# Placing the on-chip buffers of a four-layer kernel at multiples of 256 bytes

## The chip, the cores and the metric

The kernel runs on one core of one Trainium2 chip. The metric is device time in microseconds (us) from launch to end; of several runs of a kernel the median is taken. Beside it stands the profile of one execution, in which TensorE is called PE (its weight loads PEld), VectorE DVE, ScalarE ACT, GpSimd POOL, and SyncE SP. SP issues nearly all of the transfers.

## The reference

Four layers follow one another on one sequence of 2,048 rows of 640 numbers: A, B, A, B, each added to its input.

```python
x = A_x
x = x + _A_ref(_layernorm(x), A_wqkv, A_wo)
x = x + _B_ref(_layernorm(x), dft_seq_re, dft_seq_im, dft_hid_re, dft_hid_im)
x = x + _A_ref(_layernorm(x), A_wqkv, A_wo)
x = x + _B_ref(_layernorm(x), dft_seq_re, dft_seq_im, dft_hid_re, dft_hid_im)

# A: 32 heads of 20 numbers; each row looks at 8 rows: itself and 2, 4, ... 14 back
qkv = x @ wqkv                        # 640 -> 1920
logits = q . k[pos - 2 * (0..7)] * scale     # masked where pos - 2w < 0
y = softmax(logits) @ v[...] ; y @ wo        # 640 -> 640

# B: real part of a two-dimensional Fourier transform, as matrix products
a = x @ dft_hid_re.T ; b = x @ dft_hid_im.T
y = dft_seq_re @ a - dft_seq_im @ b
```

## The kernel before, in words

The sequence is cut into 4 chunks (`NC`) of 128 partitions by 4 rows (`NJ`). All matrix products are done at close to full float32 accuracy on a faster, shorter float format: each operand is split into a high part and a low part, and each product is three matmuls, high by high, high by low, low by high (`PASSES`, L222). Every matmul loads its own stationary operand (128 columns) and then streams a moving operand of 320, 480 or 512 columns past it.

Layer A (`layer_a`, L246) is a plan of steps: `at(step, phase, ...)` collects calls, and at the end they are written out step by step on all five engines in the order of `PHASES` (`manual_schedule`, so that order is the order of issue). PE computes Q, K and V for one group of rows in `qkv_mm` (L356): 15 matmuls of 480 columns, with the transposed input (tag `s0` to `s3`, one for each row j) as stationary operand and the weights of a quarter of the heads (tag `r1_0` to `r1_3`, one for each quarter q) as moving operand. The weights of a quarter are a tile `[P, 2, KD, 3 * F]`: high and low, 5 blocks of 128 inputs, 480 numbers in each. ACT copies the result out, SP stores it, and loads it again with the seven rows before it into `win` buffers. DVE does the attention: `qk_mul` (L432), `qk_red` (L442), `soft` (L455), `av_mul` (L473); POOL halves sums for it (L438, L494 to L496). The output projection is `wo_mm` (L510, matmuls at L519, 320 columns).

Layer B (`LayerB`, L892) first multiplies by the sequence matrix and then by the hidden one. The normalised rows stand as high and low parts in `self.xn[c]`, a tile `[P, 2, NJ, D]` for each chunk c in the tags `r1_0` to `r1_3`. `z_mm` (L971, matmuls at L982) makes the first of eight output tiles, at the end of layer A, and `zpart` the second at the start of layer B: `xn` is stationary and a column block of the sequence matrix (tags `s0` to `s3`, 512 columns) moves. The other six tiles are made two by two in `pair` (L1169) with seven products in place of eight (Strassen's scheme) in three loops of eight steps; `product` (L1158, matmuls at L1161) issues three passes of 512 columns for each of one or two banks. Its stationary operand comes from `x_plain` or `x_slot` (one of the chunks of `xn`); its moving operand is one of the `views`: the first part of `xn[2]`, `xn[3]` (tags `r1_2`, `r1_3`) or `s0`, `s1`. In the first loop one step is 18 matmuls; steps 0, 1, 4 and 5 take the stationary operand of two of their three products from chunk 0 (`r1_0`), steps 2, 3, 6 and 7 from chunk 1 (`r1_1`); the third product takes it from `r1_2` or `r1_3`. `ymm` (L1053, matmuls at L1064, 320 columns) multiplies by the hidden matrix: stationary `zo0`, `zo1`, `zo2`, `ot`; moving `r2a` (real part) and `pr0` to `pr3`, `zo3` (imaginary part). In `pair` the order on PE is written out; the other engines' order comes from a planner with a cost model that knows no addresses.

The buffers. `T(shape, tag)` asks one pool for a tile. Tiles of one tag share one place (or as many as `bufs` says), as large as the tag's largest tile. The pool lays the tags out in the order in which each is first asked for, each rounded up to 32 bytes of a partition. In the compiled program of the kernel before, scratch, constants, `warm`, `ident` and `nident` take the first 17,568 bytes of each partition, and the tags begin at these bytes:

| tags in order | first byte | remainder by 256 |
|---|---|---|
| ident, nident | 16544, 17056 | 160 |
| s3 | 17568 | 160 |
| mhalf, mask | 22688, 22720 | 160, 192 |
| r1_0, pr0 | 22784, 43264 | 0 |
| win, five buffers of 3,520 bytes | 48384 and on | 0, 192, 128, 64, 0 |
| pr1, pr2, pr3, r1_1, r2a, r1_2, r1_3 | 65984 to 147904 | 192 |
| zo2, zo3, ot | 168384 to 178624 | 192 |
| stats (8 of 64 bytes), junk | 183744 and on | (not read by PE) |
| s0, s1, stg (2), s2, zo0, zo1, qs, xa (2), lg (2), xr | 185536 to 226752 | 192 |

The last tag ends at byte 229,312. Every slice that PE reads begins at a multiple of 512 or 1,280 bytes inside its buffer and so has the remainder of its buffer, with one exception: the 480 numbers of a block of QKV weights are 1,920 bytes, seven and a half times 256, so that every second block is shifted by 128: in `r1_0` the blocks have the remainders 0 and 128 in turn, in `r1_1` to `r1_3` 192 and 64.

Of the kernel before, what the change touches and what calls it, by code (L numbers as in the profile page):

```python
# [11 lines left out]
F32R = mybir.dt.float32r  # L12
# [14 lines left out]
P = 128  # L27
# [2 lines left out]
NQ = 4  # L30
KD = D // P
F = 160
HQ = 8
NE = 8
FE = 80
# [20 lines left out]
NWIN = 5  # L56
# [16 lines left out]
SLOTS = NJ + W - 1  # L73
ROWS = W - 1 + S // 2
PAIRED = {NE * (NC - 1) + v: (v % NQ, v // NQ) for v in range(NE)}


@with_exitstack
def tile_layers(ctx: ExitStack, tc: tile.TileContext, x, wqkv, wo, cs, wre, wim, out):
# [10 lines left out]
    def nm(base):  # L90
        uid[0] += 1
        return f"{base}_{uid[0]}"

    def T(shape, tag, dt=F32, bufs=1, pool=None):
        return (pool or sb).tile(shape, dt, tag=tag, name=nm(tag), bufs=bufs)
# [8 lines left out]
    make_identity(nc, ident)  # L104
    nident = T([P, P], "nident", F32R)
    nc.scalar.activation(nident, ident, AF.Copy, scale=-1.0)
    zero = T([P, D], "s3", mybir.dt.bfloat16)
    nc.vector.memset(zero, 0.0)
    wb = pt([P, 512], "m1")
    for i in range(NWARM):  # L110
        nc.tensor.matmul(wb, zero[:, :P], zero[:, :512], start=True, stop=True)
    mhalf = T([P, 4], "mhalf")
    nc.gpsimd.memset(mhalf, -0.5)
    mask = T([P, SLOTS], "mask")
    nc.gpsimd.memset(mask, 0.0)
    nc.gpsimd.memset(mask[0:2, 0:3], NEG)
    nc.gpsimd.memset(mask[0:1, 3:7], NEG)
# [11 lines left out]
    def split(hi, lo, src, neg=False, eng=None):  # L129
        nc.scalar.activation(hi, src, AF.Copy, scale=-1.0 if neg else 1.0)  # L130
        if neg:
            nc.vector.scalar_tensor_tensor(lo, src, -1.0, hi.bitcast(F32), op0=ALU.mult, op1=ALU.subtract)
        else:
            (eng or nc.vector).tensor_tensor(lo, src, hi.bitcast(F32), op=ALU.subtract)
# [68 lines left out]
    def wtile(shape):  # L203
        return T(shape, "win", bufs=NWIN)

    def wq_load(q, k0, k1, tag):
        raw = T([P, k1 - k0, 3 * F], tag)
        nc.sync.dma_start(raw, wqkv[q][:, k0:k1, :])
        return raw

    def wq_load1(q, k):
        raw = wtile([P, 3 * F])
        nc.sync.dma_start(raw, wqkv[q][:, k, :])
        return raw

    def a_weights_q(q):
        wt = T([P, 2, KD, 3 * F], f"r1_{q}", F32R)
        for k in range(KD):
            split(wt[:, 0, k], wt[:, 1, k], wq_load1(q, k))
        return wt  # L220
# [25 lines left out]
    def layer_a(li, stats, handoff, prev):  # L246
# [4 lines left out]
        wq = {}  # L251
# [5 lines left out]
        qs = {}  # L257
        win = {}
# [5 lines left out]
        xr = {}  # L264
# [91 lines left out]
        def qkv_mm(g, cqj):  # L356
# [4 lines left out]
            for a, b in PASSES:  # L361
                for k in range(KD):
                    if n == (10 if g < 2 else 5):
                        for fn, args in mid.pop(g, ()):
                            fn(*args)
                    nc.tensor.matmul(mt[g][:, : 3 * F], st[:, a, k], wq[q][:, b, k], start=n == 0, stop=n == 14)  # L366
                    n += 1

        def qkv_evac(g, cqj):
            c, q, j = cqj  # L370
            if j % 2 == 0:
                sgs[q] = T([P, 6, 2, FE], "stg", bufs=2)
            nc.scalar.copy(sgs[q][:, :, j % 2], mt.pop(g)[:, : 3 * F].rearrange("p (a f) -> p a f", f=FE))  # L373

# [167 lines left out]
            nstats[c].finish(j0, j1)  # L542

        def wq_begin(q):
            wq[q] = T([P, 2, KD, 3 * F], f"r1_{q}", F32R)

        def wq_raw(q):
            if q < 3:
# [15 lines left out]
        def wq_late(q, k):  # L564
            if k == 0:
                wq_begin(q)
            wq[(q, k)] = wq_load1(q, k)
# [23 lines left out]
        def early():  # L591
# [4 lines left out]
            def w0():  # L596
                with tc.issue_after(prev.dma.ins):
                    wq[0] = a_weights_q(0)
# [32 lines left out]

        def prologue_first():
            wq_begin(0)
            for j, (k0, k1) in enumerate(((0, 3), (3, 5))):
                x_load(0, j, f"pr{j}")
# [4 lines left out]
            for q in (1, 2, 3):  # L640
                wq_begin(q)
                wq_raw(q)
# [753 lines left out]
```

## Time and profile before

| | |
|---|---|
| time, median of 3 runs | 1762.35 us (1760.95 to 1767.62) |
| span of the profiled execution, first to last instruction | 1757.1 us |
| PE, DVE, ACT, POOL busy | 1731.3, 1375.7, 807.6, 621.2 us |
| matmuls | 8,798: 1,920 at L366 (480 columns), 1,920 at L1064 and 960 at L519 (320), 2,592 at L1161 and 960 at L982 (512), the rest transposes and warm-up |
| transfers | 426.20 MB, mean 243 GB/s |

The profiled execution lies 5.2 us under the median of the runs, because a span leaves out what lies before the first and after the last instruction. The layers lie in it at about 0 to 404 us (A, its last part already belongs to B's first tile), 404 to 870 us (B), 870 to 1273 us (A) and 1273 to 1757 us (B).

A matmul's duration in the profile runs to the modelled end of its results, and one begins before the one ahead of it has ended. What a matmul costs in a stream is therefore the time from its start to the next one's start, called its pitch here: the distance of two start times in the timeline over the number of matmuls between them.

### The profile page before, as it was taken

The page shows a single profiled execution, that of the slowest core. Times are in us where ns is not written, and L with a number is a line of the kernel's source. Part 1 is how long each engine was busy: PE and PEld are TensorE (multiplying, and loading weights), DVE is VectorE, ACT ScalarE, POOL GpSimd, SP SyncE. Part 2 cuts the span into 40 slices and gives each one's busy share as a digit, 9 for nine tenths or more (in the row PEclk, how much of TensorE's full clock was granted, in tenths as well). Part 3 has the DMA queues.
Part 4 walks back from the last instruction along what each step waited for, and adds up shares of the span by engine and source line. Part 5 has one row for each costly group of instructions (what it writes and reads, how often), then busy time and mean ns, then how long its engine had stood idle before and what let it go on. Part 6 is the DMA issues. An engine that isn't in the chain of part 4 may idle for free.

```text
span 1757.1 us, 26454 instructions
## 1 busy us (share of the span) xinstructions
PE 1731.3 (99%) x8798; PEld 1501.6 (85%) x8798; DVE 1375.7 (78%) x2131; ACT 807.6 (46%) x1682; POOL 621.2 (35%) x585
## 2 busy tenths in 40 slices
PE   9999999989999999999999999989999999999999
PEld 7889897868888888888998899978788888888888
DVE  6999999988667767767648999989887677677673
ACT  4664544554445445445534434444434443443441
POOL 4799998940000000000028998889200000000000
PEclk9999999999999999999999999999999999999999
DMA  8996769759777777787657866798687767767761
GB/s 286 311 325 207 225 200 334 264 174 306 257 262 249 244 254 239 235 272 227 195 178 235 269 205 211 223 328 279 205 313 260 253 197 261 256 208 237 262 202 53
DMA packets 273961, 426.20 MB, mean 243 GB/s; under 512 B 22656, under 2 KB 153728, under 8 KB 273568
## 3 DMA queue, kind: packets, MB, share of 16 engines
q1 hardware_dynamic: 270624, 422.54, 72.7%
q10 hardware_dynamic: 3200, 1.97, 0.4%
q8 instruction: 70, 1.15, 0.3%
q14 instruction: 67, 0.55, 0.1%
HBM read 339.28 MB, written 85.14 MB: 242 GB/s over the span
## 4 chain that ended last, share of the span: by engine, by line
PE 83%; DVE 7%; DMA 4%; POOL 3%; issue 2%; ACT 1%; SPq 0%; DVEq 0%; ACTq 0%; POOLq 0%
PE m L366 20%; PE aux L1064 16%; PE t L1161 11%; PE m L1161 11%; PE pq L1161 6%; PE xt L1161 6%; PE aux L519 4%; PE t L982 3%; PE m L982 3%; DVE pr L475 2%; DMA win<-kvb 2%; PE xt L982 2%; DVE pr L435 1%; DVE lg L445 1%; POOL pr L494 1%
## 5 line engine op out<-in xcount | busy, mean ns | idle before, releaser
L366 PE MATMUL m<-r,s 128*128 128x480 f32 x1920 | 436.2, 381 | 0.7 <-DVE r L649 0.2
L366 PEld LDWEIGHTS m<-r,s 128*128 128x128 f32 x1920 | 355.5, 188 | 54.4 <-DVE r L649 1.0
L1064 PE MATMUL aux<-r2a,zo 128*128 128x320 f32 x768 | 226.6, 310 | 0.0
L1154 ACT CAST r<-win 128x512 fp32r<-128x512 f32 x246 | 149.9, 620 | 163.2 <-DVE win L1190 84.7
L494 POOL TENSOR_TENSOR pr<-pr 128x640 f32<-128x640 f32 x126 | 205.8, 1633 | 33.2 <-DVE pr L475 33.0
L1064 PE MATMUL aux<-pr,zo 128*128 128x320 f32 x704 | 208.3, 308 | 0.0
L178 POOL TENSOR_TENSOR stats<-stats,mhalf 128x1 f32<-128x1 f32 (+1 forms) x40 | 29.5, 737 | 493.4 <-ACT stats L174 484.5
L1155 DVE TENSOR_TENSOR r<-win,r 128x512 fp32r<-128x512 f32 x246 | 165.7, 688 | 45.2 <-ACT r L1154 44.1
L435 DVE TENSOR_TENSOR pr<-pq,win 128x1280 f32<-128x1280 f32 x128 | 189.8, 1483 | 13.9 <-DMA win<-kvb 8.0
L475 DVE TENSOR_TENSOR pr<-pq,win 128x1280 f32<-128x1280 f32 x128 | 190.7, 1491 | 5.1
L438 POOL TENSOR_TENSOR pr<-pr 128x640 f32<-128x640 f32 x116 | 166.3, 1434 | 16.6 <-DVE pr L435 13.6
L1161 PE MATMUL m<-r,r 128*128 128x512 f32 x594 | 152.6, 392 | 0.0
L1064 PEld LDWEIGHTS aux<-r2a,zo 128*128 128x128 f32 x768 | 144.1, 188 | 2.0
L1161 PE MATMUL t<-r,r 128*128 128x512 f32 x498 | 135.0, 392 | 0.0
L1064 PEld LDWEIGHTS aux<-pr,zo 128*128 128x128 f32 x704 | 132.2, 188 | 2.1
L1161 PEld LDWEIGHTS m<-r,r 128*128 128x128 f32 x594 | 111.4, 188 | 24.7
L982 PE MATMUL m<-s,r 128*128 128x512 f32 x384 | 118.8, 396 | 7.7 <-DMA s<-c0b 4.9
L445 DVE TENSOR_REDUCE lg<-pr 128x64 f32<-128x640 f32 (+1 forms) x128 | 112.1, 876 | 7.1 <-POOL pr L438 6.8
L982 PE MATMUL t<-s,r 128*128 128x512 f32 x384 | 117.5, 393 | 0.2 <-DVE ot L1039 0.2
L495 POOL TENSOR_TENSOR pr<-pr 128x320 f32<-128x320 f32 x126 | 112.0, 889 | 9.9
L1161 PEld LDWEIGHTS t<-r,r 128*128 128x128 f32 x498 | 93.5, 188 | 21.4
L373 ACT COPY stg<-m 128x480 f32<-128x480 f32 x128 | 70.9, 555 | 82.0 <-PE m L366 61.8
(299 smaller groups left out, 3206.0 us busy)
## 6 DMA issues: line engine op xcount, KB each, us to landing
win<-cs_in SPq DMA_DIRECT2D x351, 256.0 KB, 3.8
r<-xc SPq DMA_DIRECT2D x240, 256.0 KB, 4.1
win<-kvb SPq DMA_DIRECT2D x96, 440.0 KB, 4.4
xa<-cs_in SPq DMA_DIRECT2D x121, 256.0 KB, 3.8
win<-kvb SPq DMA_DIRECT2D x64, 360.0 KB, 4.7
kvb<-stg SPq DMA_DIRECT2D x60, 320.0 KB, 4.6
xc<-stg SPq DMA_DIRECT2D x32, 512.0 KB, 4.4
s<-c0b SPq DMA_DIRECT2D x26, 512.0 KB, 6.1
```

Of the source, the lines that this page charges most:

```text
L366: nc.tensor.matmul(mt[g][:, : 3 * F], st[:, a, k], wq[q][:, b, k], start=n == 0, stop=n == 14)
L435: nc.vector.tensor_tensor(pr, q, wview(u, jp, 0, [[1, FE]]), op=ALU.mult)
L438: nc.gpsimd.tensor_tensor(pv[:, :, 0:10], pv[:, :, 0:10], pv[:, :, 10:20], op=ALU.add)
L445: nc.vector.tensor_reduce(lgs[u][:, :, 2 * jp : 2 * jp + 2].rearrange("p h j w -> p (j w) h"), prq.pop((u, jp)), axis=AX.X, op=ALU.add,)
L475: nc.vector.tensor_tensor(pr.rearrange("p j w (h d) -> p j w h d", d=DH), lgs[u][:, :, 2 * jp : 2 * jp + 2].rearrange("p h j w -> p j w h" ...
L494: g.tensor_tensor(pr[:, :, 0:4], pr[:, :, 0:4], pr[:, :, 4:8], op=ALU.add)
L495: g.tensor_tensor(pr[:, :, 0:2], pr[:, :, 0:2], pr[:, :, 2:4], op=ALU.add)
L982: self.last = nc.tensor.matmul(self.z[t][k], self.xn[c][:, a, j, k * P : (k + 1) * P], self.ct[s][:, b], start=s == 0 and i == 0, stop=s = ...
L1064: self.last = nc.tensor.matmul(self.ym[e][:, :320], zt[(k, a, ri)][:, j2 * P : (j2 + 1) * P], w[:, e * 320 : (e + 1) * 320], start=(k, a, ...
L1154: nc.scalar.copy(hi, raw)
L1155: nc.vector.tensor_tensor(lo, raw, hi.bitcast(F32), op=ALU.subtract)
L1161: nc.tensor.matmul(bank, w(a, kb), hl[b], start=start and (a, b) == (0, 0), stop=stop and (a, b) == (1, 0),)
```

## The change

No instruction is added, removed or moved. Two things differ.

First, the addresses. `mhalf` and `mask` are asked for before the large buffers, and then a table `HOMES` asks once for every buffer of every large tag with a tile of one number that nothing writes or reads. That fixes the order of the tags. The sizes stay, so the bytes follow by adding: 17,568 + 32 + 64 = 17,664 = 69 x 256 for `s3`, and from there on each size up to `xr` (5,120, 20,480, 25,600, 512 for the eight `stats`, 1,280, 4,096, 2,560, 512) is a whole number of times 256. `s3` begins at 17664, `r1_0` at 22784 and `pr0` at 43264 as before, `pr1` at 48384, `r1_1` at 63744, `r2a` at 84224, `r1_2` at 109824, `r1_3` at 130304, `s0` at 167936, `zo0` at 191488; all have the remainder 0. `win` comes last, at 211712, with the remainders 0, 192, 128, 64, 0 that it had. `ident` and `nident` stay where they are, at 160.

Second, a quarter's QKV weights get rows of 512 numbers of which 480 are used. A block is then 2,048 bytes, and all blocks have their buffer's remainder. The tag `r1_q` does not grow: 2 x 5 x 512 numbers are the 20,480 bytes that `xn` needs there anyway.

```diff
+QPAD = 512
...
+HOMES = (
+    ("s3", 1), ("r1_0", 1), ("pr0", 1), ("pr1", 1), ("pr2", 1), ("pr3", 1), ("r1_1", 1), ("r2a", 1),
+    ("r1_2", 1), ("r1_3", 1), ("zo2", 1), ("zo3", 1), ("ot", 1), ("stats", 8), ("junk", 1), ("s0", 1),
+    ("s1", 1), ("stg", 2), ("s2", 1), ("zo0", 1), ("zo1", 1), ("qs", 1), ("xa", 2), ("lg", 2), ("xr", 1),
+    ("win", NWIN),
+)
...
+    mhalf = T([P, 4], "mhalf")
+    mask = T([P, SLOTS], "mask")
+    for tag, bufs in HOMES:
+        for _ in range(bufs):
+            T([P, 1], tag, bufs=bufs)
     zero = T([P, D], "s3", mybir.dt.bfloat16)
...
-    mhalf = T([P, 4], "mhalf")
     nc.gpsimd.memset(mhalf, -0.5)
-    mask = T([P, SLOTS], "mask")
...
     def a_weights_q(q):
-        wt = T([P, 2, KD, 3 * F], f"r1_{q}", F32R)
+        wt = T([P, 2, KD, QPAD], f"r1_{q}", F32R)[:, :, :, : 3 * F]
...
         def wq_begin(q):
-            wq[q] = T([P, 2, KD, 3 * F], f"r1_{q}", F32R)
+            wq[q] = T([P, 2, KD, QPAD], f"r1_{q}", F32R)[:, :, :, : 3 * F]
```

## The prediction

> **What bounds the kernel now.** I read the page first: span, busy times, granted clock, chain of waits.
>
> ```profile
> span 1757.1 us, 26454 instructions
> PE 1731.3 (99%) x8798; PEld 1501.6 (85%) x8798; DVE 1375.7 (78%) x2131; ACT 807.6 (46%) x1682; POOL 621.2 (35%) x585
> PEclk9999999999999999999999999999999999999999
> PE 83%; DVE 7%; DMA 4%; POOL 3%; issue 2%; ACT 1%; SPq 0%; DVEq 0%; ACTq 0%; POOLq 0%
> ```
>
> PE is busy nearly always, at the full granted clock, and 83% of the chain that ended last is PE. The average hides stages, so the next view is the table of busy time by stretch (in each row: stretch, its length, then busy time and, in brackets, instructions of PE, PEld, DVE, ACT, POOL).
>
> ```profile
> 40.00:80.00 40.00, 39.98 (x192) 34.05 (x190) 37.04 (x51) 24.11 (x59) 29.78 (x29) 1.00 0.93 308
> 200.00:240.00 40.00, 40.00 (x214) 36.02 (x213) 37.90 (x59) 16.73 (x43) 37.35 (x36) 1.00 0.65 203
> 280.00:320.00 40.00, 36.22 (x203) 31.73 (x202) 38.24 (x62) 19.52 (x52) 36.10 (x35) 1.00 0.94 331
> 600.00:700.00 100.00, 100.00 (x479) 84.79 (x478) 71.19 (x116) 48.18 (x91) 1.74 (x2) 1.00 0.76 251
> 960.00:1000.00 40.00, 40.00 (x191) 34.60 (x191) 38.32 (x53) 14.87 (x34) 38.17 (x37) 1.00 0.93 295
> 1160.00:1200.00 40.00, 37.32 (x210) 33.21 (x209) 35.19 (x56) 21.01 (x54) 37.00 (x35) 1.00 0.96 341
> 1500.00:1600.00 100.00, 100.00 (x517) 87.54 (x516) 70.59 (x117) 41.70 (x72) 0.00 (x0) 1.00 0.68 223
> ```
>
> In layer B (600 and 1500 us) PE is busy without a gap and DVE 71%: time taken from a matmul there is time taken from the kernel. In the attention stretch (40 to 240, 960 on) PE and DVE are both nearly full, with 1.7 to 3.0 us of 40 idle on DVE. In the last third of layer A (280, 1160) PE itself has gaps of 2.7 to 3.8 us in 40 while DVE, POOL and transfers are late: matmuls made faster there only wait longer.
>
> **The natural experiment in the trace.** The third view is the timeline of PE, read for pitch. This is the second half of the first loop of `pair`, steps 4 to 7 of eight; I show the rows from step 5 on (start, length, then the group).
>
> ```profile
> 484.05 1.56 PE L1161 MATMUL m<-r,r 128*128 128x512 f32 x6
> 485.44 0.86 PE L1161 MATMUL xt<-s,r 128*128 128x512 f32 x3
> 486.14 1.56 PE L1161 MATMUL t<-s,r 128*128 128x512 f32 x6
> 487.53 0.86 PE L1161 MATMUL pq<-s,r 128*128 128x512 f32 x3
> 488.23 1.55 PE L1161 MATMUL m<-r,r 128*128 128x512 f32 x6
> 489.62 0.84 PE L1161 MATMUL xt<-r,r 128*128 128x512 f32 x3
> ...
> 492.34 1.52 PE L1161 MATMUL m<-r,r 128*128 128x512 f32 x6
> 493.70 0.84 PE L1161 MATMUL xt<-s,r 128*128 128x512 f32 x3
> 494.38 1.52 PE L1161 MATMUL t<-s,r 128*128 128x512 f32 x6
> 495.74 0.84 PE L1161 MATMUL pq<-s,r 128*128 128x512 f32 x3
> 496.42 0.30 PE L1064 MATMUL aux<-r2a,zo 128*128 128x320 f32 x1
> ```
>
> Step 5 is 18 matmuls from 484.05 to 488.23: 4.18 / 18 = 232.2 ns each. Step 7 is the same 18 from 492.34 to 496.42: 4.08 / 18 = 226.7 ns. Same shape, same moving buffers (all with remainder 192 by 256); what differs is the stationary operand of 12 of the 18: step 5 has chunk 0 in `r1_0` (remainder 0), step 7 chunk 1 in `r1_1` (remainder 192). So there are two rhythms, and the fast one goes with equal remainders. The slow one outlives its cause: step 6 has `r1_1` already, and its first six matmuls still take (489.62 - 488.23) / 6 = 231.7 ns.
>
> More stretches, as stretch, length and PE busy time (the counts in the answer include neighbours that reach in; the loops themselves have 144, 168 and 150 matmuls):
>
> ```profile
> 412.46:447.41 34.95, 34.84 (x153) 1.00 0.93 322
> 463.11:496.42 33.31, 33.31 (x147) 1.00 0.78 254
> 505.23:543.89 38.66, 38.66 (x171) 1.00 0.78 253
> ```
>
> `zpart` (first row, L982, moving `s3` at remainder 160 or `s0` at 192, stationary `r1_0` to `r1_3`): 34.95 / 150 = 233.0 ns. First loop of `pair`: 33.31 / 144 = 231.3. Second loop: 38.66 / 168 = 230.1. The narrower matmuls, from the chain of waits:
>
> ```profile
> 19.52 34.70 PE m L366 x160
> 218.03 6.51 PE m L366 x30
> 631.35 8.82 PE aux L1064 x60
> 904.20 25.97 PE m L366 x120
> 959.72 22.85 PE m L366 x105
> ```
>
> At L366 (480 columns) the four rows give 90.03 us for 415 matmuls, 216.9 ns; here remainders are mixed throughout, the weight blocks alternating. At L1064 (320 columns) 8.82 / 60 = 147.0 ns with remainder 192 nearly everywhere. Between 320 columns at 147.0 and 512 at 226.7 lie 79.7 ns for 192 columns, 0.415 ns a column; so 480 columns in the fast rhythm are estimated at 147.0 + 160 x 0.415 = 213.4 ns, 3.5 under what they take.
>
> **The change part by part.** (1) `HOMES`: tiles that nobody touches make no instruction, and the planner that orders DVE, ACT, POOL and SP in `pair` knows no addresses; cost 0, no queue changes, nothing new to wait for. `mhalf` and `mask` only change their place; their memsets stay.
>
> (2) Addresses of the operands of the 512-column matmuls: all move to remainder 0, so stationary and moving agree everywhere. The trace has no stream of 512 columns with both at 0. Bounds from the nearest rows: 226.7 (both at 192) if agreement counts, 232.2 (one at 0, one at 192) if the remainder 0 itself does harm. I take 226.7: the first six matmuls of step 6 and the mixed `zpart` show the slow rhythm with and without a 0 in it, the fast one only where both agree. L1161 has 2,592 matmuls; its loops run at 230.1 to 231.3, and since the short runs between other work are like the better one I take 230.1: 3.4 x 2,592 = 8.8 us. `zpart` has 240 in each of two layers: (233.0 - 226.7) x 480 = 3.0 us. All of this lies in layer B, on the path. The 480 at L982 in layer A lie where PE has gaps: 0.
>
> (3) Padded weight rows and `s3` at L366: 1,920 matmuls x 3.5 = 6.7 us gross. The transposed inputs in `s0` to `s3` and the weights then agree in all of them. About 500 lie ahead of the full attention stretch (the 160 from 19.52 and the 120 from 904.20 among them) with DVE partly free: 1.75 us. About 1,300 lie where DVE has 2 to 3 us of 40 idle; 4.6 us gross over some 360 us could fit into that, but part of that idleness is DVE waiting for others, so I take half, 2.3 us. Together 4.0; bounds 1.7 and 6.7. When PE is early there, the next late ones are DVE and POOL, which the third row of the table already shows.
>
> (4) L1064 and L519 (320 columns): at 147.0 before; nothing to win. Where `pr0` (0) alternates with `r2a` (192) the same loop may lose a little; the row of 60 includes it and is no slower, so 0.
>
> (5) The other engines' accesses move too. DVE reads `win` at remainders 0, 192, 128, 64 and `xa` at 192:
>
> ```profile
> L1155 DVE TENSOR_TENSOR r<-win,r 128x512 fp32r<-128x512 f32 x246 | 165.7, 688 | 45.2 <-ACT r L1154 44.1
> L1155 DVE TENSOR_TENSOR r<-xa,r 128x512 fp32r<-128x512 f32 x88 | 60.4, 688 | 13.5 <-ACT r L1154 13.4
> win<-cs_in SPq DMA_DIRECT2D x351, 256.0 KB, 3.8
> xa<-cs_in SPq DMA_DIRECT2D x121, 256.0 KB, 3.8
> ```
>
> 688 ns in both, and 3.8 us to landing in both: addresses do not show on DVE or in transfers; 0. If that failed, a transfer 0.1 us later (the resolution of that row) costs nothing in layer B while its loads run a step ahead, and up to that much for each late `win` in the last third of layer A.
>
> Sum: 8.8 + 3.0 + 4.0 = 15.8 us, less relapses into the slow rhythm after each change of shape, as in step 6 (about six matmuls x 5 ns, some 40 times): 1.2. That is 14.6 us: 1757.1 - 14.6 = 1742.5 for the span; the runs' median lies 5.2 above the span, so 1762.35 - 14.6 = 1747.75, said as 1748.
>
> **A rule against it.** Row first: pitch 226.7 and 232.2 for one shape, by buffer. The Trainium skill (TensorE: Matmul & The Clock Gate, Part 2: What happens when you issue a matmul) gives PE two independent read ports and says that loading the next weights takes no read bandwidth from the running matmul; by that rule where the two operands lie cannot matter. This trace shows two rhythms, so the rule does not hold here to 5 ns, unless something else divides `r1_0` from `r1_1`; by the rule the sum is 0.
>
> **The rivals.** *No meeting of the two reads* (0.16). What divides the rhythms could be where in memory a buffer lies, not its remainder: `r1_0` (22784) and `s3` (17568) are the lowest large buffers, and they stay where they are or nearly. Against it: moving `pr0` at 43264 costs L1064 nothing. Then terms 2 and 3 fall to what the other buffers give, between 0 and 3 us: 1759 to 1762.
>
> *Remainder 0 is the slow one* (0.16; the other side). Fast needs 192, for instance because two streams that start on the same 256-byte border run into each other all along. For it: every row with a 0 in it is slow. Then all L1161 go to 232.2 (2.1 x 2,592 = 5.4 us more), the 480 at L982 in the tail cost 0 to 2.6, `zpart` stays, and L366 goes to 213.4 + 5.5 = 218.9 (2.0 x 1,920 = 3.8 more, of which PE-bound or DVE-bound, all shows, since PE would then be the late one): about 10 us, 1772. It decides once an agreeing pair at 0 takes more than the present mean of about 230 ns.
>
> *The fixed part shrinks too* (0.10). Of 226.7 ns, 512 x 0.415 = 212.5 are columns and 14 are not; if starts on a border save, say, half of that, 7 ns x 4,992 matmuls of layer B (2,592 + 480 + 1,920) are 35 us more: 1713. No row shows a matmul stream with a shorter fixed part.
>
> *Forecast* (0.58): 1743 to 1756, from all of term 3 with no relapse (8.8 + 3.0 + 6.7 = 18.5) to layer B alone with twice the relapses (11.8 - 2.4 - some of term 2 = 7).
>
> **How the numbers follow.** What a measurement of this kernel can tell from no change is about 0.5%, 8.8 us: the line lies at 1753.5. Of the forecast's 0.58, 0.06 lies above it. Faster: 0.52 + 0.10 = 0.62. Same: 0.06 + 0.16 = 0.22. Slower: 0.16. The range leaves out the shrinking fixed part below (0.08 under 1738) and most of the slow remainder above (0.12 over 1767): 1738 to 1767. The likeliest case alone has 1743 to 1756.
>
> **What would show it.** Right: steps 5 and 7 of the loop both 4.08 us; `zpart` 34.0 for 150; L366 near 213.4 (160 in 34.2); L1064 still 8.82 for 60; DVE and transfer rows unchanged; gaps on PE in the last third of layer A a little longer. Wrong: step 5 still 4.18 (place, not remainder), or step 7 at 4.18 (0 is the slow one), or L1064 under 147. It would also be wrong if PE were faster as said and the span did not follow in layer B.

## The result, and the profile after

The median is 1759.45 us (22 runs, 1752.94 to 1765.44) against 1764.09 us of the kernel before in the same session (22 runs, 1760.28 to 1767.62): ratio 0.9973, 95% interval 0.9963 to 0.9983. The change gains 4.8 us (3.0 to 6.5). The prediction had 14.6, and 1743 to 1756 us for its own case.

The page after (span, busy times, chain of waits):

```profile
span 1762.1 us, 26454 instructions
PE 1726.2 (98%) x8798; PEld 1502.0 (85%) x8798; DVE 1374.3 (78%) x2131; ACT 805.4 (46%) x1682; POOL 620.7 (35%) x585
PE 72%; DVE 10%; DMA 9%; POOL 5%; issue 3%; ACT 2%; SPq 0%; DVEq 0%; ACTq 0%; POOLq 0%
```

PE is 5.1 us less busy. This profiled execution itself took 1763.92 us, the second slowest of its 22, so its span says nothing of the gain; that of a second one (`e1_after_again`, below) is 1753.4. The profile of before errs to the other side: here and in the second profile of before a span lies 1.8 us under the time of its own execution, so the 1757.1 us belong to one of about 1758.9 (an estimate, 1757.1 + 1.8). Only 1.8 of the 5.2 us between span and median are what a span leaves out; the rest is a quick execution. What the page shows is where PE's time went: PE has lost 11 points of the chain, most of them to DVE, transfers (DMA, 4% before and 9% now) and POOL. All lines of the code stand 11 further down: L1172 is the 512-column matmul of `product` that was L1161, L993 that of `zpart` (L982), L377 that of `qkv_mm` (L366), L1075 that of `ymm` (L1064).

The first loop of `pair`, steps 5 to 7, in the timeline of PE (start, length, group):

```profile
485.01 1.52 PE L1172 MATMUL m<-r,r 128*128 128x512 f32 x6
...
489.09 1.52 PE L1172 MATMUL m<-r,r 128*128 128x512 f32 x6
490.45 0.84 PE L1172 MATMUL xt<-r,r 128*128 128x512 f32 x3
...
493.17 1.52 PE L1172 MATMUL m<-r,r 128*128 128x512 f32 x6
...
497.25 0.30 PE L1075 MATMUL aux<-r2a,zo 128*128 128x320 f32 x1
```

Steps 5, 6 and 7 all take 4.08 us, 226.7 ns a matmul, and the first six matmuls of step 6 too (490.45 - 489.09 = 1.36). The slow rhythm is gone. A whole second-loop stretch, between two blocks of `ymm` in the chain of waits (start, length, work), before and after:

```profile
1634.67 8.82 PE aux L1064 x60
...
1682.13 8.82 PE aux L1064 x60
```

```profile
1640.63 8.79 PE aux L1075 x60
...
1687.53 8.79 PE aux L1075 x60
```

From block to block it was 47.46 us and is 46.90. Less the 60 narrow matmuls (8.82 and 8.79) that leaves 230.0 and 226.8 ns for each of 168.

The 480-column matmuls did not follow. In the chain of waits after, against 25.97 us for the same 120 and 22.85 for the same 105 before:

```profile
906.90 26.02 PE m L377 x120
...
962.48 22.81 PE m L377 x105
```

That is 216.8 and 217.2 ns: nothing gained.

And in this profile PE stands still where in the first profile of before it did not. The stretch in which `zpart` runs, in either layer B, by windows (stretch, length, then busy time of PE, PEld, DVE, ACT, POOL, granted clock, which is the share of TensorE's full clock that it was granted, share of the transfer engines, GB/s), before and after:

```profile
416.00:447.00 31.00, 30.89 (x135) 24.85 (x134) 22.94 (x34) 11.87 (x23) 0.00 (x0) 1.00 0.94 323
...
1273.00:1330.00 57.00, 57.00 (x287) 49.08 (x286) 45.64 (x69) 22.39 (x40) 0.00 (x0) 1.00 0.87 305
```

```profile
416.00:447.00 31.00, 29.93 (x129) 23.52 (x128) 22.51 (x33) 12.61 (x25) 0.00 (x0) 1.00 0.96 328
...
1273.00:1330.00 57.00, 55.10 (x267) 45.89 (x266) 44.05 (x66) 21.38 (x37) 0.00 (x0) 1.00 0.88 300
```

One hole of the first stretch in the timeline after, and others further on in layer B, where `product` takes over from `ymm` (in brackets: idle time, and what ended it):

```profile
421.23 0.73 PE L993 MATMUL m<-s,r 128*128 128x512 f32 x2 [0.61 <-DVE s L980]
...
703.42 0.49 PE L1172 MATMUL xt<-r,r 128*128 128x512 f32 x1 [0.71 <-ACT r L1165]
705.23 0.74 PE L1172 MATMUL xt<-r,r 128*128 128x512 f32 x2 [1.32 <-DVE r L1166]
...
840.08 0.50 PE L1172 MATMUL xt<-r,r 128*128 128x512 f32 x1 [1.14 <-ACT r L1165]
841.23 0.74 PE L1172 MATMUL xt<-r,r 128*128 128x512 f32 x2 [0.66 <-DVE r L1166]
```

PE waits for ACT and DVE, which split column blocks of the sequence matrix into their two parts, and DVE, in the additions that make such a block (second row), waits for the blocks to arrive (group, count, busy time, mean ns, then idle time ahead of it and what ended it):

```profile
L1166 DVE TENSOR_TENSOR r<-win,r 128x512 fp32r<-128x512 f32 x246 | 165.5, 687 | 44.4 <-ACT r L1165 43.2 <-DMA r<-xc 0.3
...
L1201 DVE TENSOR_TENSOR win<-win,win 128x512 f32<-128x512 f32 x110 | 75.5, 689 | 43.4 <-DMA win<-cs_in 41.2 <-DVE zo L1050 0.8
```

DVE's operations cost what they did (687 and 689 ns). The time that the second group stood for a block to land was 37.1 us in the profile of before and is 41.2, but the second profiles, below, have 36.7 before and 35.0 after: this row names the wait and does not show that it grew.

### The profile page after: what moved, and what is told of

The parts are those of the page before. It is cut to its first block, busy times and chain, and to the rows that moved or that the text cites. A ratio compares the mean times of both kernels' runs of the same rounds, so it can differ in the third digit from the quotient of the medians.

```text
span 1762.1 us, 26454 instructions
## 1 busy us (share of the span) xinstructions
PE 1726.2 (98%) x8798; PEld 1502.0 (85%) x8798; DVE 1374.3 (78%) x2131; ACT 805.4 (46%) x1682; POOL 620.7 (35%) x585
## 4 chain that ended last, share of the span: by engine, by line
PE 72%; DVE 10%; DMA 9%; POOL 5%; issue 3%; ACT 2%; SPq 0%; DVEq 0%; ACTq 0%; POOLq 0%
PE m L377 20%; PE aux L1075 13%; PE t L1172 10%; PE m L1172 10%; PE pq L1172 5%; PE xt L1172 5%; PE aux L530 4%; DMA xc<-stg 2%; DMA win<-cs_in 2%; DVE pr L486 1%; POOL pr L505 1%; PE m L993 1%; DVE pr L446 1%; DMA win<-kvb 1%; PE t L993 1%
## 5 line engine op out<-in xcount | busy, mean ns | idle before, releaser
L377 PE MATMUL m<-r,s 128*128 128x480 f32 x1920 | 435.9, 381 | 1.8 <-ACT stg L384 1.0
L377 PEld LDWEIGHTS m<-r,s 128*128 128x128 f32 x1920 | 355.1, 188 | 55.6 <-ACT stg L384 1.6
L1075 PE MATMUL aux<-r2a,zo 128*128 128x320 f32 x768 | 226.1, 309 | 0.0
L1075 PE MATMUL aux<-pr,zo 128*128 128x320 f32 x704 | 207.8, 309 | 0.0
L1172 PE MATMUL m<-r,r 128*128 128x512 f32 x594 | 151.3, 389 | 0.0
L1075 PEld LDWEIGHTS aux<-r2a,zo 128*128 128x128 f32 x768 | 144.1, 188 | 1.9
L1075 PEld LDWEIGHTS aux<-pr,zo 128*128 128x128 f32 x704 | 132.2, 188 | 2.0
L1172 PE MATMUL t<-r,r 128*128 128x512 f32 x498 | 133.5, 390 | 0.0
L1172 PEld LDWEIGHTS m<-r,r 128*128 128x128 f32 x594 | 111.3, 188 | 23.3 <-DVE r L1166 0.5
L993 PE MATMUL m<-s,r 128*128 128x512 f32 x384 | 119.6, 399 | 11.6 <-DMA s<-c0b 5.6
L993 PE MATMUL t<-s,r 128*128 128x512 f32 x384 | 117.2, 393 | 0.2 <-DVE ot L1050 0.2
L1172 PEld LDWEIGHTS t<-r,r 128*128 128x128 f32 x498 | 93.5, 188 | 20.1
L1201 DVE TENSOR_TENSOR win<-win,win 128x512 f32<-128x512 f32 x110 | 75.5, 689 | 43.4 <-DMA win<-cs_in 41.2
```

The lines of the kernel that those rows point to most:

```text
L993: self.last = nc.tensor.matmul(self.z[t][k], self.xn[c][:, a, j, k * P : (k + 1) * P], self.ct[s][:, b], start=s == 0 and i == 0, stop=s = ...
L1075: self.last = nc.tensor.matmul(self.ym[e][:, :320], zt[(k, a, ri)][:, j2 * P : (j2 + 1) * P], w[:, e * 320 : (e + 1) * 320], start=(k, a, ...
L1172: nc.tensor.matmul(bank, w(a, kb), hl[b], start=start and (a, b) == (0, 0), stop=stop and (a, b) == (1, 0),)
```

## The experiments

Two sums are used below, both from the start times of PE's matmuls in a profile. *Excess* adds up what the intervals between two starts have above the fast rhythm (226.7 ns for 512 columns, 213.3 for 480), where that is under 17 ns in the interval. *Standing* is the same for intervals with 17 ns or more above it: PE waited, or ran at a lower clock.

**The change once more** (no edit).

> The changed kernel once more, unchanged. Theory A (equal remainders give the fast rhythm; what is won in layer B is partly given back in waits for transfers): matmuls of 512 columns again at 227 to 228 ns, those of 480 at 216.7, ratio to before 0.995 to 0.999, and PE again stalls more than before did at the starts of the 512-column loops and in zpart. Rival B (the waits in the first profile of it were that run's bad luck): the waits for transfers fall back to the level of before, and the ratio comes out at 0.994 or lower.

1759.26 us over 12 runs against 1764.23; 0.9972 (0.9959 to 0.9986). The result repeats, as theory A has it. The waits are fewer this time (see the table at the end of this section), and even so the ratio is not rival B's.

**Is it the remainder 0, or agreement?** `win` goes to the front of the table, so that all buffers that PE reads lie at 192:

```diff
 HOMES = (
+    ("win", NWIN),
     ("s3", 1), ("r1_0", 1), ...
-    ("win", NWIN),
 )
```

> Same as the changed kernel, but the window buffers stand first in the order, so that every buffer that TensorE reads lies at remainder 192 and not 0. Theory A (agreement counts, not the value): 512 columns at 227 to 228 ns in all steps, 480 at 216.7, time as the changed kernel's within 0.2%. Rival C (remainder 0 is itself good or bad for matmuls): pitch differs from the changed kernel's by 2 ns or more. Rival D (transfers to and from buffers at remainder 0 are slower than at 192, which eats the gain): pitch the same, but xa and c0b loads land 0.2 to 0.4 us sooner than in the changed kernel and the ratio to before is 0.994 or lower.

In its chain of waits (its lines stand one higher, L1074 for L1075):

```profile
1638.33 8.79 PE aux L1074 x60
...
1685.23 8.79 PE aux L1074 x60
```

46.90 us as with 0, so rival C is out. The time, 1757.2 us (0.9962; 0.9946 to 0.9978), is 2 us under the changed kernel's, within the noise, and not at rival D's 0.994; its `xa` loads land after 4.0 us (4.1 and 3.7 in the two profiles after), those from `c0b` after 5.7 (6.5 and 6.3), so a small part of rival D is not excluded. The other side: `win` between `r1_1` and `r2a`, so that `s3`, `r1_0`, `r1_1`, `pr0` to `pr3` lie at 0 and the rest at 192, and stationary and moving operand of nearly all 512-column matmuls differ:

```diff
-    ("r1_1", 1), ("r2a", 1),
+    ("r1_1", 1), ("win", NWIN), ("r2a", 1),
...
-    ("win", NWIN),
```

> The window buffers stand in the middle of the order: s3, r1_0, r1_1, pr0 to pr3 at remainder 0; r2a, r1_2, r1_3, s0 to s2, zo and ot at 192. So stationary operands from chunks 0 and 1 disagree with every 512-column moving operand. Theory A: steps 5 and 7 of the first loop both at 4.18 us, L1161's counterpart at 231 to 233 ns in nearly all rows, some 4 to 8 us more than before in layer B, ratio to before 1.002 to 1.005. Rival E (the place of r1_0 low in memory counts, not remainders): step 5 at 4.18 us and step 7 at 4.08 us as before, ratio 1.000.

```profile
1645.15 8.80 PE aux L1074 x60
...
1693.04 8.74 PE aux L1074 x60
```

Here it is 47.89 us, and (47.89 - 8.80) / 168 = 232.7 ns. In the first loop steps 5 and 7 both take 4.18 us (485.24 to 489.42 and 493.61 to 497.79), step 7 with `r1_1` as stationary buffer, which was fast before: rival E, the place in memory, is out. The excess at the line of `product` is 15.8 us over 2,592 matmuls, where it was 8.8 before and is 1.4 after. The kernel takes 1769.75 us, 1.0027 (1.0014 to 1.0040) of before: 5.5 us slower. For 512 columns agreement decides, not the value and not the place.

**The two halves of the change.** Only the table, weight rows of 480 numbers as before:

```diff
-QPAD = 512
+QPAD = 480
```

> The changed order of buffers without the padding of the QKV weight rows: weight blocks at remainders 0 and 128 in turn, stationary s0 to s3 at 0. Theory A as corrected by the profile of the changed kernel (480 columns take 216.7 ns whatever the remainders): 480 columns at 216 to 218 ns, time equal to the changed kernel's within 0.2%. Rival F (the padding does give 480 columns something): they take 2 ns more than in the changed kernel, the kernel 1 to 4 us more.

1758.39 us, 0.9968 (0.9954 to 0.9983): all that is gained, the table gains. The padding makes the 480-column matmuls slower: their excess is 5.1 us without it and 6.6 with it (7.0 before), 216.1 and 216.9 ns.

**The pitch by itself.** A kernel of nothing but PE streams: 50 matmuls with a weight load each, at chosen remainders of stationary and moving operand, after a few narrow ones.

```python
def stream(bank, n, s, m, count):
    for i in range(count):
        so = ((i % 5) * 512 + s) // 4
        mo = (4096 + (i % 5) * 2048 + m) // 4
        nc.tensor.matmul(bank[:, :n], wide[:, so : so + P], wide[:, mo : mo + n], start=True, stop=True)
```

> Nothing but streams of 50 matmuls each on PE, with the input as data (the output is not computed: the input is stored in its place): column counts 512, 480, 448, 384, 320, 256, stationary and moving operand at remainders by 256 that agree (0, 32, 64, 128, 192) or differ. Theory A: 512 columns 226.7 ns where both agree, whatever the value, and 230 to 236 where they differ by 32, 64, 128 or 192; a difference of 256 counts as agreement. 480 columns 216.7 in all pairs, since 1,920 bytes are no whole number of times 256; 448, 384, 320, 256 columns at agreement 200.0, 173.3, 146.7, 120.0. Rival C (the value counts): agreement at 64 or 128 is slow.

512 columns with both operands at 64, with both at 32, with one at 0 and one at 32; 480 with both at 0 (start, length, group of the timeline):

```profile
48.13 11.55 PE L107 MATMUL acc<-wide 128*128 128x512 f32 x50
...
73.06 11.61 PE L107 MATMUL acc<-wide 128*128 128x512 f32 x50
...
85.57 11.89 PE L107 MATMUL acc<-wide 128*128 128x512 f32 x50
...
212.56 11.05 PE L107 MATMUL acc<-wide 128*128 128x480 f32 x50
```

Once a stream has settled, its start times give 226.7 ns for 512 columns wherever the two agree by 256 (0, 32, 64, 128, 192, and 0 with 256), and 228.9 to 233.4 where they do not. 320 and 384 columns do not care whether the distance is 0 or 64 (146.7, 173.3). But 480 columns take 216.6 ns where they agree, and 448 columns are slower there (206.7) than 64 bytes apart (200.0): my expectation for the narrower widths was wrong. So the distance was walked in steps of 16 bytes:

> Again only PE streams of 50 matmuls with a weight load each; the layers are left out and the input is stored as the output. For 480, 448 and 512 columns the moving operand's remainder by 256 bytes is walked from 0 to 240 in steps of 16, the stationary one at remainder 0. Theory 1, a meeting of the two reads that depends on the distance of their addresses: for 512 columns only the distance 0 is at 226.7 ns and all others lie between 228 and 234; for 480 columns some distance other than 0 reaches 213.3 ns (520 - 8 cycles, the fixed part of 32 that 512 has), as 448 did at 64 with 200.0; then term 3 of the prediction was sized for a distance that 480 columns do not like. Theory 2, 480 columns have a fixed part of their own (40 cycles, 216.7 ns) at best: every distance gives 216.5 to 218.5, and no placing of the weights can bring term 3.

For 512 columns only the distance 0 has 226.7; the 15 others have 231.1 to 236.7. (At 64 it is 233.3 here, and was 228.9 in the kernel of streams before this one: away from 0 the distance does not settle the rhythm alone.) For 480 columns the 16 distances give 213.3 to 220.0: 216.7 at 0, and 213.3 at 112 and 144 alone. The streams that counted were then run five times each, entered after 4 to 16 narrow matmuls:

> Again only PE streams of 50 matmuls with a weight load each, the layers left out and the input stored as the output. Each distance that counted is run five times, with 4, 7, 9, 13 and 16 narrow matmuls ahead of the stream, so that it is entered differently: 480 columns at the distances 0, 112, 144, 64, 192; 448 at 0 and 64; 512 at 0 and 192. Theory 1, the distance decides: all five streams of a distance have one pitch, 213.3 ns for 480 at 112 and 144, 216.7 at 0, 200.0 for 448 at 64, 226.7 and 233.3 for 512 at 0 and 192. Theory 2, the rhythm that a stream falls into depends on how it is entered as well: the five differ by 2 ns or more for 480 and 448, and the 213.3 ns at 112 and 144 was luck; only 512 at 0 is at 226.7 in all five.

480 at distance 0 (one of five), at 112 (one), at 144 (a slow one, and the one fast one), then 512 at 0 (one) and at 192 (first and last):

```profile
22.97 11.04 PE L105 MATMUL acc<-wide 128*128 128x480 f32 x50
...
117.96 10.89 PE L105 MATMUL acc<-wide 128*128 128x480 f32 x50
...
141.61 11.21 PE L105 MATMUL acc<-wide 128*128 128x480 f32 x50
...
177.72 10.90 PE L105 MATMUL acc<-wide 128*128 128x480 f32 x50
...
433.46 11.56 PE L105 MATMUL acc<-wide 128*128 128x512 f32 x50
...
495.78 11.87 PE L105 MATMUL acc<-wide 128*128 128x512 f32 x50
...
547.46 11.87 PE L105 MATMUL acc<-wide 128*128 128x512 f32 x50
```

Both theories hold in part. All five agree for 480 at 0 (216.7), 64 (218.3 to 218.4), 112 (213.3) and 192 (216.0), for 448 at 64 (200.0), for 512 at 0 (226.7) and 192 (233.3). At other distances the way in counts: 480 at 144 settles at 213.3 once and at 217.8 to 220.0 four times, 448 at 0 at 202.7 once and 206.7 four times.

**Would faster 480-column matmuls have shown?** In the kernel after, each padded weight row is begun 28 numbers in, 112 bytes:

```diff
+QOFF = 28
...
-F32R)[:, :, :, : 3 * F]
+F32R)[:, :, :, QOFF : QOFF + 3 * F]
```

> The kernel after the change, with the 480 weights of each padded row begun at its 28th number, so that moving and stationary operand of every 480-column matmul lie 112 bytes apart by 256 (the distance at which the scan had 213.3 ns). The rest lies as after the change. Theory 1, term 3 failed only because 480 columns have their fast rhythm at another distance: L367 and its kin fall from 216.9 to 213.5 ns, 6.5 us of PE time in layer A, and the median falls by 2 to 6 us against the kernel after the change (to 1753 to 1757; ratio to before 0.994 to 0.996). Theory 2, the rhythm is not kept in the kernel, where blocks of 15 matmuls are cut by others: 216 to 218 ns and no change (ratio 0.996 to 0.998). Theory 3, 480 columns get faster but layer A is bound by DVE and POOL where they run: pitch 213.5, ratio 0.996 to 0.998 all the same.

The same two rows of the chain, between two more that stand for the same matmuls in both kernels; first this kernel, then the one after the change:

```profile
862.93 3.38 PE m L378 x15
...
907.07 25.67 PE m L378 x120
...
962.18 22.65 PE m L378 x105
...
1057.82 3.22 PE m L378 x15
```

```profile
862.85 3.25 PE m L377 x15
...
1058.59 3.26 PE m L377 x15
```

120 matmuls take 25.67 us (213.9 ns) in place of 26.02; the excess over all 1,920 falls from 6.6 to 2.6 us. From the first to the last of the rows shown it is 194.89 us against 195.74 in the kernel after: 0.85 us gained in the first 200 us of the second layer A. The kernel takes 1759.28 us, 0.9967 (0.9955 to 0.9980): no different from the change as it stands. These are the numbers of theory 3; that DVE and POOL are what holds layer A is its argument, and no run here takes work from them.

**Where did layer B's gain go?** The kernel before once more (no edit), and both kernels without the stores and loads of the parked stationary products (`x_combine`, `x_slot`), which are 84 of 426 MB:

> The kernel before once more, for a second profile of its waits. In its first profile the 512-column matmuls of layer B stood still for only 3 us, in those of the changed kernel and its variants for 7 to 14 us. Theory A (a faster PE runs into its transfers): 2 to 5 us again. Rival G (the first profile was a quiet run, and the waits vary by themselves): 7 us or more.

> The kernel before without the stores to and the loads from xc in layer B (272 transfers, some 80 of 426 MB; two of the five loads in each step of the first two loops): the products take the plain chunks in place of the combined ones, so the result is another. Theory A: the pitch stays at 230 ns, the waits nearly vanish, and the time falls by 0 to 6 us. It is the base for the next run.

> The changed kernel without the same transfers (xc stored and loaded nowhere in layer B). Theory A (what is won in the matmuls of layer B is lost again in waits for transfers that are near their limit there): with the load of transfers taken away the whole gain shows, 9 to 12 us under the previous run (ratio of the two 0.993 to 0.995), and the 512-column matmuls stand still for under 3 us in the loops. Rival H (the gain is lost elsewhere, in layer A or by the clock): the difference of the two stays at 4 to 6 us.

```diff
-            if apart:
-                for h, v in enumerate((hi, lo)):
-                    nc.sync.dma_start(self.xc[m][:, i : i + 2, h], v.bitcast(F32))
-            else:
-                nc.sync.dma_start(self.xc[m][:, i : i + 2], hl.bitcast(F32))
...
-            nc.sync.dma_start(v.bitcast(F32), self.xc[m][:, i])
```

1757.06 us (12 runs; 0.9976 of before with all transfers, 0.9961 to 0.9991) and 1747.09 (6 runs; 0.9918, 0.9896 to 0.9939): the change is now worth 10.0 us. The windows of the kernel after, without these transfers:

```profile
416.00:447.00 31.00, 31.00 (x139) 25.68 (x138) 26.46 (x41) 13.96 (x24) 0.00 (x0) 1.00 0.38 116
...
1273.00:1330.00 57.00, 57.00 (x282) 49.22 (x281) 44.02 (x71) 22.12 (x39) 0.00 (x0) 1.00 0.33 103
```

PE stands nowhere in them, with transfers at a share of 0.38 and 0.33. (In four other comparisons with all transfers, the unchanged kernel after, all at 192, the table only and the weights at 112, the gain was 5.0, 7.0, 5.8 and 4.8 us.) The runs draw together too: the 17 runs of before in that session spread over 13.7 us (1755.58 to 1769.27), the 12 without these transfers over 4.6. The single execution of before that was profiled again took 1766.19 us, and its PE stood for 9.8 us in layer B, where the first profile of before had 2.9. That is rival G: the first profile was a quiet one, and the kernel before waits too, by chance more or less. The windows of the second profiles, before and then after, no longer differ:

```profile
416.00:447.00 31.00, 30.57 (x131) 23.92 (x130) 22.16 (x33) 12.41 (x24) 0.00 (x0) 1.00 0.93 327
...
1273.00:1330.00 57.00, 56.49 (x274) 47.67 (x273) 44.88 (x67) 21.03 (x36) 0.00 (x0) 1.00 0.89 307
```

```profile
416.00:447.00 31.00, 30.76 (x133) 24.11 (x132) 23.34 (x34) 10.97 (x19) 0.00 (x0) 1.00 0.93 317
...
1273.00:1330.00 57.00, 56.55 (x280) 47.70 (x279) 45.59 (x69) 22.37 (x40) 0.00 (x0) 1.00 0.87 300
```

So no pair of single profiles shows that the change makes PE wait; that rests on the runs with fewer bytes.

The pair was then measured again, and with transfers added, 128 KB from memory to memory behind each of the 240 loads in the queue (the expectation says ahead):

```diff
             nc.sync.dma_start(v.bitcast(F32), self.xc[m][:, i])
+            nc.sync.dma_start(self.sink[m][:, i], self.xc[m][:, i, 0])
```

> The kernel before without the stores and loads of the parked stationary products in layer B (the same stale buffers are multiplied instead, so the result is another). Both theories: 1755 to 1759, 0.996 to 0.9985 of before.

> The kernel after the change, with the same stores and loads left out. Theory 1, about half of the ten microseconds that PE gained in layer B is given back as waits for transfers: 8 to 11.5 us under the kernel before with the same left out (ratio of the two 0.9935 to 0.9955), against 4.8 us with all transfers. Theory 2, the waits of single profiles are chance and the six runs of the first such measurement were lucky: 3.5 to 6 us under it (0.9965 to 0.998), as with all transfers.

> The kernel before, with one more transfer of 128 KB (from memory to memory, read by nobody) ahead of each of the 240 loads of parked products in layer B: 31.5 MB more. Slower than before by some 2 to 20 us, since the start of layer B and its first loop already keep the transfers busy at a share above 0.9.

> The kernel after the change, with the same transfers added. Theory 1, transfers take the gain back: still less of it is left than the 4.8 us with the usual transfers, 0 to 3 us under the kernel before with the same added (ratio of the two 0.998 to 1.000). Theory 2, the gain of 4.8 us does not hang on transfers: 4 to 6 us (0.9965 to 0.9975).

Without the transfers 1756.64 and 1748.34 us (0.9964, 0.9951 to 0.9977, and 0.9912, 0.9892 to 0.9932, of before): 8.3 us, theory 1, near the lower end of its range. With more transfers 1822.94 and 1818.93 us (1.0332, 1.0307 to 1.0356, and 1.0311, 1.0288 to 1.0333): 4.0 us, between the 0 to 3 of theory 1 and the 4 to 6 of theory 2; five runs each, spread over 8.2 and 4.7 us, cannot tell the two apart. The expected price was far off as well (61 us in place of 2 to 20), and PE's longest waits, before and after, say why:

```profile
PE t L1164 <- ACT s L1157: 15.5, 2, 9.4
```

```profile
PE t L1175 <- ACT s L1168: 15.3, 2, 9.6
```

A few waits of up to 9.6 us, the same in both kernels; and the granted clock of these ten runs is 0.984 to 0.989, against 0.995 to 1.000 in all others, which comes to at most some 18 of the 61 us (an estimate: a hundredth of 1,820). The pair shows large stops that no speed of PE touches, not a little less room for transfers. That more transfers take more of the gain is not shown.

Leaving transfers out takes away bytes and entries of SP's queue at once. So the last pair keeps every entry and cuts its bytes:

```diff
-                    nc.sync.dma_start(self.xc[m][:, i : i + 2, h], v.bitcast(F32))
+                    nc.sync.dma_start(self.xc[m][:, i : i + 2, h, :64], v[:, :, :64].bitcast(F32))
...
-                nc.sync.dma_start(self.xc[m][:, i : i + 2], hl.bitcast(F32))
+                nc.sync.dma_start(self.xc[m][:, i : i + 2, 0, :64], hl[:, :, 0, :64].bitcast(F32))
...
-            nc.sync.dma_start(v.bitcast(F32), self.xc[m][:, i])
+            nc.sync.dma_start(v[:, 0, :64].bitcast(F32), self.xc[m][:, i, 0, :64])
```

> The kernel before, with every store and load of parked products kept in its place in the queue, but cut to 64 numbers a row of one of the two parts (32 KB a load in place of 256; the rest of the buffer is stale, so the result is another). Both theories: 1755 to 1761, near the kernel without them.

> The kernel after the change with the same cut. Theory 1, what takes the gain back is the bytes that transfers have to move: 8 to 11 us under the kernel before with the same cut (ratio of the two 0.994 to 0.9955), as without these transfers. Theory 2, it is their number and their order in SP's queue, whose issue waits for the stores and for free buffers: the gain stays near that with all transfers, 4 to 6 us (0.9965 to 0.9975).

1758.12 and 1750.06 us (0.9970, 0.9958 to 0.9983, and 0.9920, 0.9900 to 0.9940): 8.1 us, at the lower end of theory 1's range. With every queue entry in its place it is the bytes that make the difference. Alone this pair is weak (6 and 12 runs, spread over 7.4 and 6.2 us); the three pairs, 10.0, 8.3 and 8.1, agree. Whether the bytes act by crowding the loads of the sequence matrix, or because the loads that were cut land sooner themselves, these runs do not separate. The clock is not the reason: the mean granted clock of the 22 runs after is 0.998, as in the runs of before.

All together, by the two sums (us; the 512-column matmuls of layer B, 3,004 of them in the parts counted):

| kernel | profiles | excess in layer B | standing in layer B |
|---|---|---|---|
| before | 2 | 10.5, 10.5 | 2.9, 9.8 |
| fast rhythm (after twice, all at 192, table only, weights at 112) | 5 | 1.7 to 1.9 | 13.2, 7.4, 14.4, 9.3, 11.1 |
| operands differ | 1 | 17.3 | 8.0 |
| before, transfers left out or cut | 3 | 10.5 | 1.3, 1.3, 2.2 |
| after, transfers left out or cut | 3 | 1.4 to 1.5 | 1.6, 1.2, 4.7 |

The excess falls by 8.7 us, and every profile agrees on it. The standing rises from 6.3 (mean of two, which lie 7 us apart) to 11.1 (mean of five), by 4.7, and moves by 1 to 3 us with where the parts are taken to begin. That 8.7 - 4.7 = 4.0 lies near the 4.8 measured is in part luck: in layer A the five profiles have about 3 us less excess and 5 us more standing than the two, and with these the sum is 2, which is also what the mean spans of the seven differ by (1760.8 and 1758.6). What is given back is sized better by the pairs without the bytes.

## Why the prediction was right and wrong

*Step 1 (the table costs nothing):* nothing in a profile speaks against it.

*Step 2 (512 columns), mechanism right, size a little high:* forecast 8.8 + 3.0 us of PE time in layer B, less 1.2 of relapses, 10.6. Excess at `product` fell from 8.82 to 1.37 us, by 7.45; with the matmuls of `z_mm` and `zpart` in layer B it is the 8.7 of the table. All of `z_mm` and `zpart` together fell from 3.91 to 1.14, but most of this lies ahead of layer B, where the step had booked nothing: of the 240 matmuls of `zpart` in each layer only 180 run in layer B, the other 60 at the end of layer A. Steps 5 and 7 at 4.08 us came as said; with agreement at 192 and with disagreement the kernel moved to either side as the mechanism wants.

*"All of this lies in layer B, on the path":* this step failed. I had read 100.00 of 100.00 us busy in 600 to 700 (and in 1500 to 1600) and took it for all of layer B; in step 5 I wrote that its loads run a step ahead. Behind PE stand ACT and DVE, and behind those the transfers, which my own fence had at a share of 0.93 in `zpart`. A faster PE asks for its column blocks sooner than they land, and part of the gain turns into waits. With the parked products' bytes gone the same change is worth 10.0, 8.3 and 8.1 us; with them 4.8. So 3 to 5 us of step 2 were given back to transfers. That the bytes take it is shown by leaving them out; the way from landing to wait is read from the waits of single profiles, and argued.

*Step 3 (480 columns), size wrong:* 6.7 us gross were forecast and 4.0 taken; the excess fell by 0.4, and the kernel without the padding does as well. The estimate drew a line from 320 to 512 columns and took agreement to be the fast place at every width. It is not for 480: there agreement has 216.7 ns and 112 bytes have 213.3. The second half of the step was too high as well: with the weights at 112, 4.0 us of PE time were won and the median did not move. In layer A as a whole, PE stood 41.7 and 42.2 us before and 43.9 to 50.6 in the five profiles of the fast rhythm: what it gains there it seems to wait.

*Step 4 (320 columns, 0):* right, 8.79 for 60. *Step 5 (DVE and transfers, 0):* right for DVE, 687 ns. Landing times of single groups moved by 0.1 to 0.4 us,

```profile
win<-cs_in SPq DMA_DIRECT2D x351, 256.0 KB, 3.9
...
xa<-cs_in SPq DMA_DIRECT2D x121, 256.0 KB, 4.1
```

but they are 3.9 and 3.7 in the second profile of the same kernel, and the second of before has 3.8 and 4.1: two profiles of one kernel differ as much, and no effect of the address is to be seen.

*The rivals.* "No meeting of the two reads" is refuted by step 5 and by the disagreeing kernel; "remainder 0 is the slow one" by 46.90 us at 0 as at 192; "the fixed part shrinks" by the 226.7 ns that steps 5 to 7 have, which is what the fast step 7 had before. What the prediction drew from the Trainium skill's two independent read ports (TensorE: Matmul & The Clock Gate, Part 2: What happens when you issue a matmul), that it cannot matter where the operands lie, does not hold here: in the streams by themselves the same shape takes 226.7 and 233.3 ns by address alone.

*The sum.* Of the 14.6 us, the 4.0 of step 3 did not come, step 2 was 1.9 too high (10.6 and 8.7), and about 4.0 went into waits for transfers (8.8, the mean of the three pairs without the bytes, less 4.8). That leaves 4.7; that it meets the 4.8 so closely is luck, since the last term is uncertain by some 2 us. The prediction itself had named this failure, PE faster as said and the span not following in layer B, but gave it no price. Its outer range, 1738 to 1767, holds the measured time only because it was drawn wide enough for other cases; the forecast's own 1743 to 1756 does not.

## What to carry to other kernels

Pitch is read from start times, and two pitches for one shape are worth a look at the addresses of both operands. Before a gain on PE is booked, look behind it in the same stretch, at who feeds PE and how full the transfers are: here, with shares of 0.94 and 0.87 in two stretches, 3 to 5 of some 9 us turned into waits, and with 0.38 and 0.33 hardly any did. The price is the gain without some of those bytes less the gain with them. One profile of each kernel is not enough for it: the waits of two profiles of one kernel lay 7 us apart. Which distance is the fast one is a matter of the width; measure it for the width at hand in a stream by itself.

## What the runs showed that I had not expected

Whether a 512-column matmul with its weight load runs in the fast rhythm hangs on the distance of its two operands by 256 bytes: 226.7 ns at 0 and 229 to 237 at any other of 15. For 448 and 480 columns the fast distances are others (16, 64 and 160; 112), and at some the stream settles in one of several rhythms by the way it is entered.

A short wait can cost more than itself. Toward the end of the second layer A, in the first profile after, PE waited 2.74 us for a transfer, and then:

```profile
1165.66 1.22 PE L993 MATMUL m<-s,r 128*128 128x512 f32 x2 [2.74 <-DMA s<-c0b]
1166.68 0.63 PE L993 MATMUL xt<-s,r 128*128 128x512 f32 x1
...
1170.09 1.91 PE L342 MATMUL aux<-ident,zo 128*128 128x128 f32 x8
```

Ten matmuls took 4.43 us, 443 ns each in place of 227: 2.2 us more. The granted clock over that stretch:

```profile
1160.00:1180.00 20.00, 16.92 (x80) 14.32 (x80) 13.04 (x21) 7.79 (x20) 14.05 (x15) 0.83 0.88 338
```

The mean granted clock is 0.83 there, and 0.50 from 1165.6 to 1170.0, the ten matmuls. The Trainium skill (TensorE: Matmul & The Clock Gate, Part 1: The HAM clock gate) halves the clock after about 3.4 us without work, by a window that runs freely; the trace agrees on the half (0.50), and here 2.7 us of waiting were enough. In the first profile of before PE waited 2.33 us for the same load, and the clock stayed at 1.00.

Open is why PE stood some 5 us longer in layer A, mean of five against two; the five profiles after lie up to 7 us apart among themselves.
